# Decode attention with two branches on one core: normalization and output projection moved from the end into earlier heads

## The chip, the cores and the metric

The kernel runs on one core of one Trainium2 chip. The metric is the device time in microseconds (us); lower is better. The runs of one kernel lie close together (the twelve of the kernel before between 876.38 and 877.85 us, 0.2%), and most of the differences here lie between that and 1%. So kernels that are compared were timed in rounds against the kernel before, on the same chip.

A profile is one execution. Its span, from the first to the last instruction, is about 1.8 us shorter than the time measured for the same execution (2.4 us in one profiled run, `e6_same_pe_time`).

## The reference

There are two branches, A and B. Each is one decode step of attention with 32 heads of width 128, and each has its own input, caches and weights. A attends to all 16384 keys, B to the last 4096. The two results, 512 numbers each, are set side by side.

```python
def _A_ref(x, k_cache, v_cache, wq, wo):          # B is the same with
    ...                                           # k_cache[:, :, Sk - 4096:, :] and v alike
    q = (x @ wq).reshape(B, Sq, Hq, Dh).transpose(0, 2, 1, 3)
    scores = jnp.einsum("bhqd,bhkd->bhqk", q, k) * (Dh ** -0.5)
    p = _softmax(scores, axis=-1)
    o = jnp.einsum("bhqk,bhkd->bhqd", p, v)
    return o.transpose(0, 2, 1, 3).reshape(B, Sq, Hq * Dh) @ wo
...
return jnp.concatenate([a, b], axis=-1)
```

The K and V that must be read are 8 MB per A head and 2 MB per B head. With four weights of 4 MB, 336 MB go from memory into the core. (These MB are of 2^20 bytes; the profile counts in millions of bytes and shows 352.)

## The kernel before

A and B heads alternate: A0, B0, A1, B1, and so on, 64 in all; I call them heads 0 to 63, so that head 62 is the last A head and head 63 the last B head. A transfer brings one "unit", up to 64 blocks of 128 keys (2 MB), into a slot of a ring: five slots for K, four for V. All transfers go through one DMA queue, issued by SyncE (SP), and before each one SP waits until its slot is free.

For an A head PE transposes K in 16 groups of eight blocks, ACT copies each group from PSUM, and PE multiplies it with q. For a B head DVE forms the scores. ACT takes the exponential, and PE multiplies it with V (`ov`) in column `hidx` of the bank `OL[b]`; the sum of the exponentials goes to column 32 + `hidx`, in partition 0 only.

```python
for hh in range(NH):                       # PE
    ...
    if br == "A":
        for u in head_units[hh]:
            pe.wait_ge(s_k[ks], 16 * kocc[u])
            for gi in range(ugroups[u]):
                transposes(u, gi)
                if len(lag) >= 2:
                    scores(*lag.pop(0))
                lag.append((u, gi))
        while lag:
            scores(*lag.pop(0))
    if hh >= 1:
        ov(hh - 1)
ov(NH - 1)
```

Only after the last head are the sums inverted, broadcast by PE from partition 0 to all, copied and multiplied. Then come 32 products of 512 columns for A and 32 for B. A's output weights wo have lain in the weight buffer since head 6. B's wo (4 MB) is the last transfer of all and goes into two used slots of the K ring.

```python
# SP, after the last V
sp.dma_start(wob_view[:, :, :], B_wo.rearrange("(c p) n -> p c n", p=128)).then_inc(s_w, 16)
...
# PE, after the last head
pe.wait_ge(dve_m, DM_LINV)
...                                        # broadcast of the 64 inverse sums
pe.wait_ge(dve_m, DM_ONORM)
pe.wait_ge(s_w, 48)
for h in range(HQ):
    ins = pe.matmul(outA_ps, onorm[:, h : h + 1], wo_view[:, h, :], start=(h == 0), stop=(h == HQ - 1))
ins.then_inc(pe_fin, 1)
pe.wait_ge(s_w, 64)
for h in range(HQ):
    ins = pe.matmul(outB_ps, onorm[:, HQ + h : HQ + h + 1], wob_view[:, h, :], ...)
```

The softmax here doesn't subtract the row's maximum and nothing guards it: scores larger than these inputs give would overflow.

## Time and profile before

The time before was 877.49 us in three runs. The profiled run took 878.35 us, a little more than usual, with a span of 876.6 us.

| event before | us from the start |
|---|---|
| last V landed (all 16 completions) | 853.96 |
| attention of the last head done | 855.2 |
| last byte, B's wo: half of the completions, all 16 | 852.3, 864.75 |
| A's projection | 857.62 to 867.36 |
| B's projection | 867.36 to 874.28 |
| end of the span | 876.6 |

From the page of the kernel before: the busy share of the DMA engines and the rate they moved in 40 equal slices of 21.9 us, the queues (packets, MB, share of the 16 engines' time), and the chain of waits by engine.

```profile
span 876.6 us, 29290 instructions
DMA  7999799999999999999999999999999999999992
GB/s 289 422 428 384 300 385 425 426 424 424 422 424 424 424 425 423 426 425 424 423 424 425 424 424 425 425 424 423 420 425 410 423 422 422 408 425 413 419 360 77
q1 hardware_dynamic: 38082, 352.34, 96.3%
q8 instruction: 108, 1.77, 0.8%
DMA 79%; PE 14%; issue 3%; ACT 2%; DVE 2%; SPq 0%; ACTq 0%
```

The DMA engines are busy in nearly every slice, mostly at about 424 GB/s, and 79% of the chain is transfers. This kernel is limited by the bytes it reads: without B's wo the last V came 11.6 us earlier (`e4_no_wob`). Work of PE beside the transfers costs little (63 us more of it in the middle cost 0.7 us, `e6_same_pe_time`); what costs time is the work in the last slice, which moves 77 GB/s.

The end of the chain of waits before, in order of time (start, duration, what):

```profile
825.44 0.85 PE ol L483 x26
826.29 2.00 issue
828.29 1.18 PE ol L483 x38
...
829.98 23.98 DMA vring<-in_B_v_cache_dram
853.96 0.14 issue
854.10 0.99 PE ol L483 x32
...
857.62 9.74 PE misc L534 x32
867.36 6.92 PE misc L544 x32
874.28 0.02 issue
874.30 0.68 DVE out_sb L357
```

After the last V, 22.6 us pass, most of them in the two projections (L534 is A's, L544 is B's). B's products are faster: the granted clock rises from 0.5 to 1.0 at 863.06, and the starts of the products, 0.427 us apart before it, are then 0.216 us apart. B's wo is not in the chain: it landed at 864.75, while A's projection was running. The line of 2.00 us of "issue" in the middle of a run of 64 products: PE stood still there though the profile shows nothing that it waited for.

### The profile page before, as it was taken

The numbers are of one execution on the slowest core, as the hardware profiler recorded it, in microseconds if no ns is written. First come the engines' busy times: TensorE is split into PE (matmuls) and PEld (weight loads), VectorE is DVE, ScalarE is ACT, GpSimd is POOL, SyncE is SP. The second block draws the span as 40 slices with busy tenths as digits, with TensorE's granted clock in tenths as the row PEclk, the third lists the DMA queues.
The fourth block names the chain that finished last, engine by engine and source line by source line (L and its number), as shares of the span: only waits on it lengthen the run. The fifth ranks groups of instructions, "written<-read, shape, count | busy, mean of one in ns | idle before, by whom it ended". The sixth has DMA issues, their size and how long they took to land.

```text
span 876.6 us, 29290 instructions
## 1 busy us (share of the span) xinstructions
PE 648.8 (74%) x13764; PEld 569.8 (65%) x13764; DVE 223.8 (26%) x87; ACT 498.6 (57%) x641; POOL 0.7 (0%) x6
## 2 busy tenths in 40 slices
PE   1846885787777677778676787786767877777778
PEld 1745784676666666667665676776766766766673
DVE  0017303333112333331133333212333332123331
ACT  0603773677555556766555677655556776555660
POOL 0000000000000000000000000000000000000000
PEclk9956876788777688877677787766678786667778
DMA  7999799999999999999999999999999999999992
GB/s 289 422 428 384 300 385 425 426 424 424 422 424 424 424 425 423 426 425 424 423 424 425 424 424 425 425 424 423 420 425 410 423 422 422 408 425 413 419 360 77
DMA packets 38203, 354.21 MB, mean 404 GB/s; under 512 B 4289, under 2 KB 12481, under 8 KB 12482
## 3 DMA queue, kind: packets, MB, share of 16 engines
q1 hardware_dynamic: 38082, 352.34, 96.3%
q8 instruction: 108, 1.77, 0.8%
q14 instruction: 13, 0.11, 0.0%
HBM read 352.32 MB, written 0.00 MB: 402 GB/s over the span
## 4 chain that ended last, share of the span: by engine, by line
DMA 79%; PE 14%; issue 3%; ACT 2%; DVE 2%; SPq 0%; ACTq 0%
DMA vring<-in_A_v_cache_dram 72%; PE ol L483 7%; DMA wbuf<-in_B_wq_dram 3%; DMA vring<-in_B_v_cache_dram 3%; ACT kts L373 2%; PE misc L430 2%; DMA wbuf<-in_A_wq_dram 2%; PE ktp L447 1%; PE misc L534 1%; PE misc L544 1%; DVE qb_sb L300 1%; PE ol L491 1%; DVE sbb L324 1%; PE misc L409 0%; SPq L201 0%
## 5 line engine op out<-in xcount | busy, mean ns | idle before, releaser
L373 ACT ACTIVATE kts<-ktp 128x1024 bf16<-128x1024 bf16 x512 | 475.4, 1077 | 266.9 <-PE ktp L447 266.3
L447 PE MATMUL ktp<-ident,kring 128*128 128x128 bf16 x4096 | 361.8, 245 | 73.8 <-DMA kring<-in_A_k_cache_dram 73.4
L447 PEld LDWEIGHTS ktp<-ident,kring 128*128 128x128 bf16 x4096 | 286.2, 111 | 79.0 <-DMA kring<-in_A_k_cache_dram 76.9
L463 PE MATMUL sba<-qT_sb,kts 128*128 128x1 bf16 x4096 | 183.4, 166 | 69.9 <-ACT kts L373 42.2
L463 PEld LDWEIGHTS sba<-qT_sb,kts 128*128 128x128 bf16 x4096 | 149.4, 99 | 127.2 <-ACT kts L373 126.2
L315 DVE TENSOR_TENSOR prd<-kring,qb_sb 128x4096 bf16<-128x4096 bf16 x32 | 73.4, 2292 | 560.0 <-DMA kring<-in_B_k_cache_dram 559.8
L483 PE MATMUL ol<-ebuf,vring 128*128 128x1 bf16 x5120 | 150.8, 165 | 45.7 <-DMA vring<-in_A_v_cache_dram 35.3
L483 PEld LDWEIGHTS ol<-ebuf,vring 128*128 128x128 bf16 x5120 | 143.1, 103 | 50.0 <-DMA vring<-in_A_v_cache_dram 34.6
L324 DVE TENSOR_REDUCE sbb<-prd 128x32 f32<-128x4096 bf16 x32 | 141.4, 4420 | 1.1
L394 ACT ACTIVATE ebuf<-sbb 128x32 bf16<-128x32 f32 x32 | 7.3, 230 | 68.0 <-DVE sbb L324 52.1
L430 PE MATMUL misc<-wbuf,xrep 128*128 128x128 bf16 x128 | 15.1, 312 | 13.4 <-DMA wbuf<-in_B_wq_dram 7.9
L430 PEld LDWEIGHTS misc<-wbuf,xrep 128*128 128x128 bf16 x128 | 13.0, 146 | 15.3 <-DMA wbuf<-in_B_wq_dram 8.0
L381 ACT ACTIVATE ebuf<-sba 128x128 bf16<-128x128 f32 x32 | 8.9, 277 | 14.5 <-PE sba L463 14.5
L300 DVE CAST qb_sb<-misc 128x512 bf16<-128x512 f32 x8 | 5.5, 692 | 45.1 <-PE misc L430 45.1
L409 PE MATMUL misc<-xT_sb,wbuf 128*128 128x1 bf16 x128 | 3.6, 165 | 18.2 <-DMA wbuf<-in_A_wq_dram 18.2
L409 PEld LDWEIGHTS misc<-xT_sb,wbuf 128*128 128x128 bf16 x128 | 3.5, 104 | 18.2 <-issue 18.2
L491 PE MATMUL ol<-rowsum,ones_col 128*1 128x1 f32 x128 | 12.2, 164 | 3.1 <-issue 3.1
L534 PE MATMUL misc<-wbuf,onorm 128*1 128x512 bf16 x32 | 9.7, 479 | 0.7 <-DVE onorm L348 0.7
L534 PEld LDWEIGHTS misc<-wbuf,onorm 128*1 128x1 bf16 x32 | 3.1, 100 | 6.9 <-issue 3.9
L544 PE MATMUL misc<-kring,onorm 128*1 128x512 bf16 x32 | 7.1, 379 | 0.0
L491 PEld LDWEIGHTS ol<-rowsum,ones_col 128*1 128x1 f32 x128 | 5.5, 80 | 2.3 <-issue 1.3
L381 ACT ACTIVATION_READ_ACCUMULATOR ebuf<-sba 128x1 f32 x32 | 6.2, 194 | 0.0
(23 smaller groups left out, 16.6 us busy)
## 6 DMA issues: line engine op xcount, KB each, us to landing
kring<-in_A_k_cache_dram SPq DMA_DIRECT2D x64, 2048.0 KB, 28.5
vring<-in_A_v_cache_dram SPq DMA_DIRECT2D x64, 2048.0 KB, 22.6
kring<-in_B_k_cache_dram SPq DMA_DIRECT2D x32, 1024.0 KB, 28.8
vring<-in_B_v_cache_dram SPq DMA_DIRECT2D x32, 1024.0 KB, 33.6
wbuf<-in_A_wq_dram SPq DMA_DIRECT2D x1, 4096.0 KB, 13.6
wbuf<-in_B_wq_dram SPq DMA_DIRECT2D x1, 4096.0 KB, 29.5
wbuf<-in_A_wo_dram SPq DMA_DIRECT2D x1, 4096.0 KB, 31.4
kring<-in_B_wo_dram SPq DMA_DIRECT2D x1, 4096.0 KB, 34.2
```

The costliest lines, as they stand in the source:

```text
L300: v.tensor_copy(qb_sb[:, bch * 4 * DH : (bch + 1) * 4 * DH], misc7[:, 0 : 4 * DH],).then_inc(dve_m, 1)
L315: v.tensor_tensor(PRD[:, :].rearrange("p (c d) -> p c d", d=DH), Kring[:, ks * UC : ks * UC + TB, :], qb_bcast(hb), op=ALU.mult,).then_inc ...
L324: v.tensor_reduce(SBB[hb % 2][:, 0:TB], PRD[:, :].rearrange("p (c d) -> p c d", d=DH), AXX, ALU.add,).then_inc(dve_red, 1)
L373: act.activation(KTs[g % NS][:, 0 : GS * 128], KTP[g % NKB][:, 0 : GS * 128], ACTF.Copy,).then_inc(act_ev, 1)
L381: act.activation(Ebuf[e][:, 0:TA], SBA[:, 0:TA], ACTF.Exp, bias=0.0, scale=inv_sqrt_dh, accum_out=rowsum[e][:, 0:1],).then_inc(act_ex, 1)
L430: last = pe.matmul(misc7[:, i * DH : (i + 1) * DH], xrep[:, jc, :], wq_view[:, jc, hb * DH : (hb + 1) * DH], start=(jc == 0), stop=(jc == ...
L447: last = pe.transpose(KTP[g % NKB][:, t * 128 : (t + 1) * 128], Kring[:, ks * UC + c, :], ident[:, :],)
L463: last = pe.matmul(SBA[:, c0 + c : c0 + c + 1], KTs[g % NS][:, t * 128 : (t + 1) * 128], qT_sb[:, a_rank[hh] : a_rank[hh] + 1], start=True ...
L483: pe.matmul(OL[b][:, hidx : hidx + 1], Vring[:, vs * UC + c, :], Ebuf[e][:, c0 + c : c0 + c + 1], start=first, stop=(c0 + c == T - 1),)
L491: pe.matmul(OL[b][0:1, HQ + hidx : HQ + hidx + 1], ones_col[:, 0:1], rowsum[e][:, 0:1], start=True, stop=True,).then_inc(pe_ov, 1)
L534: ins = pe.matmul(outA_ps, onorm[:, h : h + 1], wo_view[:, h, :], start=(h == 0), stop=(h == HQ - 1),)
L544: ins = pe.matmul(outB_ps, onorm[:, HQ + h : HQ + h + 1], wob_view[:, h, :], start=(h == 0), stop=(h == HQ - 1),)
```

## The change

The intent is to leave nearly nothing after the last head. The sums are formed with a full 128x128 matrix of ones, so that each partition has them and the broadcast goes. Heads are normalized and projected in batches of eight. A's products run among the 16 groups of A heads 22, 38, 54 and 62, B's among those of 30, 46 and 62, and seven of B's within `ov` of head 62; only the last head of each branch is left for the end. B's wo comes in four transfers of 1 MB: three replace chunks of A's wo that are used up, after heads 22, 38 and 54, and the fourth is issued before the last three V transfers.

```diff
+                def issue_wob(k):
+                    if k < 3:
+                        sp.wait_ge(pe_pa, k + 1)
+                        dst = wo_view[:, k * CH : (k + 1) * CH, :]
+                    else:
+                        ...                      # wait for the last use of K slot 1
                 for hh in range(NH):
                     for u in head_units[hh]:
                         dma_k_unit(u)
+                    if hh == NH - 1:
+                        issue_wob(3)
+                    for k in range(3):
+                        if hh == 16 * k + 26:
+                            issue_wob(k)
...
-                sp.dma_start(wob_view[:, :, :], B_wo...)         # after the last V
...
                     pe.matmul(
-                        OL[b][0:1, HQ + hidx : HQ + hidx + 1],
-                        ones_col[:, 0:1],
+                        OL[b][:, HQ + hidx : HQ + hidx + 1],
+                        ones_mat[:, :],
                         rowsum[e][:, 0:1],
...
+                        if hh == NH - 2 and c0 > 0:              # in ov
+                            pe.wait_ge(dve_n, N_B3)
+                            pe.wait_ge(s_wb[3], 16)
+                            for h in range(3 * CH, HQ - 1):
+                                project(1, h)
...
+                for k in range(3):
+                    extra[16 * k + 22] = ([(dve_n, N_AB[k]), (s_w, 48)],
+                        [(0, h) for h in range(CH * k, CH * (k + 1))], True)
+                    extra[16 * k + 30] = ([(s_wb[k], 16)],
+                        [(1, h) for h in range(CH * k, CH * (k + 1))], False)
+                waits_, todo_, _f = extra[NH - 2]
+                extra[NH - 2] = (waits_ + [(dve_n, N_A3)],
+                    todo_ + [(0, h) for h in range(3 * CH, HQ - 1)], False)
...
                                 transposes(u, gi)
+                                if todo:
+                                    p = project(*todo.pop(0))
...
-                ...                              # broadcast, 32 products of A, 32 of B
+                pe.wait_ge(dve_n, N_A31)
+                project(0, HQ - 1).then_inc(pe_fin, 1)
+                pe.wait_ge(dve_n, N_B31)
+                project(1, HQ - 1).then_inc(pe_fin, 1)
```

## The prediction

> **What bounds it.** The DMA queue. The page's slices show the DMA engines at 0.9 or more in 37 of 40, mostly at about 424 GB/s; 79% of the chain of waits is DMA, and PE waits only 73 us for A's K and 35 us for A's V (waits). So the input stream ends when its bytes are in, whatever their order: the last packets end at 864.3 us. Half of the engines finish 12 us earlier (landings of the last transfer: 8th at 852.3, last at 864.8). The instruction queue (q8: 108 packets of 16 KB[...]) would explain that lag. The instruction count hardly changes, so I expect the lag to stay.
>
> **The end before.** B's wo (4 MB) comes last. The last V lands at 853.96; attention ends at 855.2; reciprocals, broadcast and scaling take until 857.6; A's projection 9.74 us, B's 6.92, the copy 0.68, the store and its receipt 1.6 (timeline, chain). So 22.6 us follow the last V, 12 us the last byte.
>
> **What changes.** The bytes stay, but V of the last head is now last: it should land where wo did, at 864.8, or up to 0.7 us later, because 1 KB packets take 51 instead of 46 ns while larger ones run (packets of the trace). 62 of the 64 projections move to earlier heads, where ACT paces PE (0.92 us per group against 0.65 of PE work) or PE waits for DMA. They cost 0.427 us each at half clock, 0.216 at full (starts of the 512-column products[...]). The DMA queue's new waits (projections of heads 22, 38, 54; last use of slot 1) are met before the queue reaches them, or with the wait beside them. The f32 sums over 128 columns cost about 0.5 instead of 0.19 us per head (estimate from the f32 broadcast, 0.53 each): +20 us of PE, hidden.
>
> **The new end.** K of the last A head lands some 26 us before the last V (23.7 before, plus 1 MB at 2.5 us), about 838.6. Its groups take 16.3 us plus 2 to 3 for 15 projections; then B's head 1.3, half of A's V 1.9, seven projections 1.5 to 3.0, the other half 1.9 + 0.5: 864.8 to 865.6. So PE and the last V (864.8 to 865.5) meet. Then last head 1.0, sum 0.5, normalization 0.5, projection 0.5, copy 0.7 (0.25 more behind A's copy on DVE), store 1.6: 870 to 871.5 of span. The measured time is 0.9 above the span: **predicted 871.2 us, 868.5 to 874.5 in 8 of 10**, a gain of 0.7%. Faster by over 2%: 0.01; within 2%: 0.97; slower: 0.02. About 17 of the 22.6 us go, but 11 come back, because the last V lands later.
>
> **Right or wrong.** Right if the last V lands at 864 to 866, the chain ends in it or in PE's last two heads, and DMA slices stay at about 424 GB/s. Wrong if the DMA has new holes after heads 26, 42, 58 or 63; if the last V lands before 862; or if PE's last A head takes over 3 us longer from its K than 16.3.
>
> **What could make it wrong.** A new stall near a wo chunk; a lower clock in the tail; another count of instruction packets on the lagging engines, which moves the end of the stream.

## The result, and the profile after

The changed kernel is correct. Its median is 873.53 us in ten runs (873.01 to 874.54) against 877.21 us. The ratio is 0.9958, with a 95% interval of 0.9949 to 0.9967: 0.4% faster, within 2%. The time lies in the predicted range, 2.3 us above the predicted value.

The same parts of the page for the changed kernel:

```profile
span 871.2 us, 29301 instructions
DMA  7999799999999999999999999999999999999995
GB/s 303 422 426 384 290 385 425 426 422 427 421 426 422 424 424 425 424 393 424 424 424 424 427 422 426 422 367 429 425 425 424 423 422 425 426 405 386 426 389 231
q1 hardware_dynamic: 38130, 352.34, 96.9%
q8 instruction: 108, 1.77, 0.8%
DMA 66%; PE 23%; ACT 4%; issue 4%; DVE 1%; SPq 1%; ACTq 0%
```

The bytes and the instruction packets are the same. The dips to 393, 367 and 386 GB/s are where the three chunks of wo pass. They are more than slow packets: in SP's timeline the transfer behind each chunk, a V of B, took 24.1, 22.1 and 23.2 us to issue, which the profile counts as issuing and not as a wait for a semaphore (0.43 us for the first of them in the run below without B's wo). Meanwhile the half of the DMA engines that is ahead (a reading of the completions, see "Which engines set the last byte") seems to have run out of work: the DMA share is 0.85 from 780 to 792 us, 1.01 in the kernel before. The half that is behind, which sets the last byte, went on: behind each chunk the ninth completion of V came 2.46 to 2.50 us after that of the chunk, as is usual for 1 MB (mostly 2.45 to 2.50 us in the kernel before). The last slice now carries 231 GB/s instead of 77: transfers go on nearly to the end. In the chain, PE has gained most of what the DMA lost.

The end of the chain in the changed kernel, with the head's K landing at its top:

```profile
811.75 28.11 DMA kring<-in_A_k_cache_dram
839.86 0.25 issue
840.11 1.01 PE ktp L482 x8
841.12 0.51 PE misc L508
...
845.78 0.47 PE ktp L482 x8
846.25 0.31 PE misc L508
846.56 0.28 PE sba L498 x8
...
857.95 1.03 ACT kts L408
858.98 0.05 issue
859.03 0.35 PE sba L498 x8
859.38 0.80 PE ol L535 x32
...
862.05 2.89 PE misc L508 x7
864.95 1.69 PE ol L535 x64
866.63 0.22 PE ol L543 x2
866.86 0.80 PE ol L535 x32
...
868.34 0.60 PE misc L508
868.96 0.68 DVE out_sb L392
```

From the landing of K at 839.86 to the end the chain is almost all PE's, with no further transfer in it. `misc L508` is a projection. One group of the last A head takes 0.47 + 0.31 + 0.28 = 1.06 us here; seven projections of B (2.89 us, at a granted clock of 0.5 until 864.63) stand between the two halves of A's V.

| us from the start, in the profiled runs | before | after |
|---|---|---|
| last V landed | 853.96 | 864.99 |
| last byte of any input | 864.75 | 864.99 |
| from the last V to the end | 22.6 | 6.2 |
| end of the span | 876.6 | 871.2 |

So 16.4 us of the tail went, and 11.0 us came back because the last V lands later: what used to come after it, B's wo, now comes before it. Where the last byte lands hardly moved. Of the remaining 5.4 us, 1.7 us are the sample: the profiled run before was 1.1 us above its median, and that of the changed kernel 0.5 us below its own. That leaves the 3.7 us between the medians.

### The profile page after: what moved, and what is told of

The parts are those of the page before. It is cut to its first block, busy times and chain, and to the rows that moved or that the text cites. A ratio compares the mean times of both kernels' runs of the same rounds, so it can differ in the third digit from the quotient of the medians. Undisturbed runs are those within 1.5% of the kernel's fastest.

```text
span 871.2 us, 29301 instructions
## 1 busy us (share of the span) xinstructions
PE 663.0 (76%) x13760; PEld 576.8 (66%) x13760; DVE 225.9 (26%) x100; ACT 503.7 (58%) x641; POOL 0.7 (0%) x6
## 2 busy tenths in 40 slices
DMA packets 38251, 354.21 MB, mean 407 GB/s; under 512 B 4337, under 2 KB 12529, under 8 KB 12530
## 4 chain that ended last, share of the span: by engine, by line
DMA 66%; PE 23%; ACT 4%; issue 4%; DVE 1%; SPq 1%; ACTq 0%
DMA vring<-in_A_v_cache_dram 40%; DMA kring<-in_A_k_cache_dram 21%; PE ol L535 7%; PE ktp L482 7%; ACT kts L408 4%; DMA wbuf<-in_B_wq_dram 3%; PE misc L508 3%; PE sba L498 2%; PE misc L465 2%; PE ol L543 2%; DMA wbuf<-in_A_wq_dram 1%; DVE qb_sb L342 1%; SPq L247 1%; DVE sbb L366 1%; PE misc L444 0%
## 5 line engine op out<-in xcount | busy, mean ns | idle before, releaser
L408 ACT ACTIVATE kts<-ktp 128x1024 bf16<-128x1024 bf16 x512 | 480.4, 1069 | 262.7 <-PE ktp L482 260.8
L482 PE MATMUL ktp<-ident,kring 128*128 128x128 bf16 x4096 | 357.7, 243 | 67.0 <-DMA kring<-in_A_k_cache_dram 62.8
L482 PEld LDWEIGHTS ktp<-ident,kring 128*128 128x128 bf16 x4096 | 281.1, 109 | 74.6 <-DMA kring<-in_A_k_cache_dram 51.6
L498 PEld LDWEIGHTS sba<-qT_sb,kts 128*128 128x128 bf16 x4096 | 146.5, 98 | 131.3 <-ACT kts L408 126.9
L535 PE MATMUL ol<-ebuf,vring 128*128 128x1 bf16 x5120 | 149.1, 165 | 40.5 <-DMA vring<-in_A_v_cache_dram 31.6
L535 PEld LDWEIGHTS ol<-ebuf,vring 128*128 128x128 bf16 x5120 | 146.6, 103 | 44.0 <-DMA vring<-in_A_v_cache_dram 28.2
L543 PE MATMUL ol<-rowsum,ones_mat 128*128 128x1 f32 x128 | 33.5, 331 | 0.0
L543 PEld LDWEIGHTS ol<-rowsum,ones_mat 128*128 128x128 f32 x128 | 29.5, 286 | 0.0
L508 PE MATMUL misc<-wbuf,onorm 128*1 128x512 bf16 x56 | 24.5, 438 | 0.0
L315 DVE RECIPROCAL linv<-ol 128x8 f32<-128x8 f32 (+2 forms) x10 | 2.0, 196 | 33.3 <-PE ol L543 33.3
L508 PEld LDWEIGHTS misc<-wbuf,onorm 128*1 128x1 bf16 x56 | 4.4, 79 | 7.4 <-issue 3.5
```

The lines of the kernel that those rows point to most:

```text
L408: act.activation(KTs[g % NS][:, 0 : GS * 128], KTP[g % NKB][:, 0 : GS * 128], ACTF.Copy,).then_inc(act_ev, 1)
L482: last = pe.transpose(KTP[g % NKB][:, t * 128 : (t + 1) * 128], Kring[:, ks * UC + c, :], ident[:, :],)
L498: last = pe.matmul(SBA[:, c0 + c : c0 + c + 1], KTs[g % NS][:, t * 128 : (t + 1) * 128], qT_sb[:, a_rank[hh] : a_rank[hh] + 1], start=True ...
L508: return pe.matmul((outA_ps, outB_ps)[b], onorm[:, b * HQ + h : b * HQ + h + 1], wo_view[:, h, :] if b == 0 else wob_head(h), start=(h == ...
L535: pe.matmul(OL[b][:, hidx : hidx + 1], Vring[:, vs * UC + c, :], Ebuf[e][:, c0 + c : c0 + c + 1], start=first, stop=(c0 + c == T - 1),)
L543: pe.matmul(OL[b][:, HQ + hidx : HQ + hidx + 1], ones_mat[:, :], rowsum[e][:, 0:1], start=True, stop=True,).then_inc(pe_ov, 1)
```

## The experiments

Twelve kernels were run. The questions were what sets the last byte's time, whether PE or the last V ends the changed kernel, which part of the change bought the time, and what limits a version without its weak points.

### PE's work in the last A head

```diff
-                waits_, todo_, _f = extra[NH - 2]
-                extra[NH - 2] = (waits_ + [(dve_n, N_A3)],
-                    todo_ + [(0, h) for h in range(3 * CH, HQ - 1)], False)
+                extra[NH - 4] = extra.pop(NH - 2)
...
+                        if hh == NH - 2:         # before the first transpose
+                            pe.wait_ge(dve_n, N_A3)
+                            for h in range(3 * CH, HQ - 1):
+                                project(0, h)
```

> The changed kernel with the 15 projections taken out of the last A head's groups: A's seven (heads 24 to 30) run before its first transpose, where PE waited 4.2 us for K, and B's eight of chunk 2 move one A head earlier. Theory 1 (PE ends the changed kernel, 2 us after the last V): the last A head's groups go back to about 16.3 us from 19.4, PE waits for the last V again, and the time falls by 1.0 to 1.8 us. Theory 2 (the last V alone sets the end, PE's extra work is hidden): no change, within 0.4 us.

Median 872.0 us, ratio to the kernel before 0.9945 (0.9933 to 0.9958), so about 1.1 us faster than the changed kernel. The two intervals overlap, so the size is uncertain; the profiled spans, 870.2 and 871.2 us, differ by about as much. In its timeline the groups of the last A head take 16.3 us, from 841.72 to 857.99, as expected. But the seven products before them ran from 838.64 to 841.79 and so past K's landing at 838.60, and the seven of B still took 3.1 us (granted clock 0.61 from 858 to 866). PE began the last head 0.9 us after its V had landed (865.99 against 865.13). The direction of theory 1 is supported: PE's late work was part of the end. The statement that PE waits for the last V again was not reached.

### B's wo at the end after all, in four transfers

A's early projections and all normalizations are kept. B's wo follows the last V as in the kernel before, but in four parts, and PE projects each part as it lands.

```diff
-                    if hh == NH - 1:
-                        issue_wob(3)
-                    for k in range(3): ...
...
+                for k in range(NCH):             # after the last V; NCH = 4, CW = 8
+                    sp.dma_start(wob_view[:, k * CW : (k + 1) * CW, :],
+                        B_wo[k * CW * DH : (k + 1) * CW * DH, :].rearrange("(c p) n -> p c n", p=128)
+                    ).then_inc(s_wb[k], 16)
...
                 pe.wait_ge(dve_n, N_B31)
-                project(1, HQ - 1)
+                for h in range(HQ - 1):
+                    if h % CW == 0:
+                        pe.wait_ge(s_wb[h // CW], 16)
+                    project(1, h)
+                project(1, HQ - 1)
```

A's products for heads 24 to 30 also run before the last A head's first transpose, as in the run above, so this is not the single part alone.

> One part of the change alone: A's projections and all normalizations early, but B's wo stays at the end of the stream as before, in four transfers of 1 MB, and B's projections follow at the end as each chunk lands. Theory 1 (bytes set the end of the stream, and only the work after the last byte counts): the last chunk lands at 864 to 866 as in both kernels, eight products of 0.22 to 0.43 us, copy and store follow, and the span ends at 869.5 to 871.5, as fast as the changed kernel or 1 us faster, so that moving B's wo forward gained nothing. Theory 2 (the gain comes from taking wo off the end of the stream): 2 us or more slower than the changed kernel.

Median 870.89 us, ratio 0.9933 (0.9919 to 0.9946): the fastest correct kernel, together with its variant below, and faster than the changed one, whose interval is 0.9949 to 0.9967. Against the run above the intervals overlap. The end of its chain:

```profile
853.17 11.27 DMA kring<-in_B_wo_dram
864.44 0.04 issue
864.48 1.90 PE misc L498 x8
866.39 0.02 issue
866.41 0.68 DVE out_sb L382
```

The last V lands at 853.17 (853.96 before), the last byte at 864.44 (864.75 before), and 4.3 us follow to the end at 868.7, a little below the span that theory 1 gave. Moving B's wo forward was therefore not needed. What counts is how little work stands behind the last byte, whichever tensor it belongs to.

### B's wo at the end, in one transfer

The same with `NCH = 1`.

> As the run with B's wo last in four transfers, but as one transfer of 4 MB, as in the kernel before, so that none of B's 32 products can start before its last byte. Theory 1 (only the work after the last byte counts): last byte at 864.8, then 32 products at 0.22 to 0.25 us, copy and store: a span of 873.5 to 875.5, so 2 to 3 us better than before and 5 us worse than in four transfers. Theory 2 (taking A's projection off the end gives its full 9.7 us): a span of 867 to 868.

Median 877.51 us, ratio 1.0005 (0.9991 to 1.0018): no gain over the kernel before. Both expectations missed. The end of its chain:

```profile
828.50 35.95 DMA kring<-in_B_wo_dram
864.45 0.14 issue
864.58 9.41 PE misc L498 x32
873.99 0.02 issue
874.02 0.68 DVE out_sb L382
```

The last byte is where theory 1 has it, but B's 32 products take 9.41 us where they took 6.92 us before. PE had been idle for 8.86 us before them. The granted clock had been 0.5 since 848.86, before this wait began, and stayed there until 869.34. In the kernel before it was at 0.5 from 845.99, but A's projection filled the wait, and the clock rose at 863.06.

### The same with a busy PE

```diff
                 pe.wait_ge(dve_n, N_B31)
+                for _t in range(26):             # results unused
+                    pe.matmul(OL[0][:, 0:512], ident[:, :], qb_sb[:, 0:512], start=True, stop=True)
```

> The run with B's wo last in one transfer, with 26 dummy products of 512 columns (into scratch PSUM) while PE waits some 9 us for wo. There the 32 products took 9.41 us, at a granted clock of 0.5 until 5 us after they began, where before they took 6.92 us. Theory 1 (PE's idle wait lowered its clock, and this ate what A's early projection had gained): the products take 6.9 to 7.3 us and the time falls by 2.1 to 2.5 us, to about 875.2. Theory 2 (wo's rows in the K ring or something else is slow): no change.

Median 876.21 us, ratio 0.9983 (0.9971 to 0.9996), by the ratios 1.9 us faster than without the dummy products. The chain's end:

```profile
828.47 36.08 DMA kring<-in_B_wo_dram
864.55 0.04 issue
864.60 7.08 PE misc L498 x32
```

The same 32 products now take 7.08 us, with the clock at 1.0 from 861.05. So the idle wait had kept the clock at half and taken back the gain of the early projection. It had not lowered the clock, as theory 1 has it: the clock fell at 848.86, 6.9 us before that wait began, with PE at work on the last heads (in the kernel before, where it fell at 845.99, PE had been busy 2.99 of the 4.00 us before that), and why it fell then is not shown. The rise came 4.0 to 5.5 us after the first of the products of 512 columns in six profiled runs: the kernel before, this one, and B's wo last in one part, in four equal parts and in the two uneven divisions below.

### Smaller last parts

```diff
-        NCH = 4
-        CW = HQ // NCH
+        WB = (0, 14, 24, 30, 32)
```

> The kernel with B's wo last, its four transfers cut as 14, 10, 6 and 2 heads instead of 8 each. Theory 1 (only the work after the last byte counts): 2 products instead of 8 follow the last byte, 0.5 to 0.9 us instead of 1.90, so 0.9 to 1.4 us faster than with four equal ones: a median of 869.5 to 870.1. Theory 2 (the last byte itself comes later with uneven chunks, or the clock drops while PE waits): no gain.

Median 872.38 us, ratio 0.9939 (0.9926 to 0.9953): no gain, theory 2. The first part, 14 heads, landed at 859.30 instead of 855.86. PE started 3.4 us later, with the products 0.43 us apart until 864.0, and ran all 32 without a pause in 9.29 us, until 868.73; the last byte at 865.63 no longer mattered.

With `WB = (0, 8, 16, 26, 32)`:

> The kernel with B's wo last, in transfers of 8, 8, 10 and 6 heads: the first ones as in the run with four equal ones, so that PE starts and warms as early as there, and 6 products in place of 8 after the last byte. Also a second sample of that version. Theory 1 (the small last chunk failed because the large first one let PE begin 3.4 us later, at half clock): as fast as four equal transfers or up to 0.5 us faster, a ratio to the kernel before of 0.9925 to 0.9940, the last 6 products in 1.3 to 1.5 us. Theory 2 (uneven chunks delay the last byte): about 1.2 us slower, as with 14, 10, 6 and 2.

Median 871.07 us, ratio 0.9927 (0.9913 to 0.9940). That agrees with four equal parts and is a second sample of that version on another occasion. Its profiled run was the slowest of its five (872.38 us): its last byte came at 866.64, and its last 16 products, which began at 864.67, took 3.63 us, so that the time of the last 6 alone can't be read.

### Bytes or work?

The changed kernel without any transfer of B's wo; B's products read A's wo, so B's result is wrong.

```diff
                 def issue_wob(k):
+                    return
...
-                            pe.wait_ge(s_wb[3], 16)
...
-                        [(s_wb[k], 16)],
+                        [],
...
-                        wo_view[:, h, :] if b == 0 else wob_head(h),
+                        wo_view[:, h, :],
```

> The changed kernel without any transfer of B's wo (B's products read A's wo: a wrong result for B on purpose). Theory 1 (bytes on the DMA set the time): 4 MB fewer, on the lagging engines 256 descriptors of 1 KB each at 43 to 47 ns, 11 to 12 us less. Theory 2 (the stream has slack, PE or the ring's waits set the pace): under 4 us less.

Median 864.64 us, ratio 0.9864 (0.9850 to 0.9877), by the ratios 8.2 us faster than the changed kernel. The last V landed at 853.36 instead of 864.99, 11.6 us earlier, as theory 1 says. The time fell less than its 11 to 12 us, because 9.4 us instead of 6.2 us followed the last V. Without the megabyte between them, the last A head's K and the last V come closer together (22.5 us apart instead of 25.1), and PE's chain from K to the end takes its time all the same. Again PE is last in this kernel.

### Which engines set the last byte

In the kernel before and in the one with B's wo in four parts, half of the completions of the last transfers come early. The last V of the kernel with B's wo in four parts had its first completion at 838.20, the eighth at 839.16 and the last at 853.17. The distance grows through the kernel, from about 1.5 us at 90 us to 15 us. I read the 16 completions of a transfer as one from each of the 16 DMA engines, so that half of the engines would be ahead of the others. The trace does not tell which engine moved a packet. The suspect was the fetching of instructions: 108 packets of 16 KB on the instruction queue, median 1.07 us each. (The kernel before has 27528 PE instructions, 255 for each packet.) My estimate: spread over eight engines that is 13.5 packets each, 14 us.

More instructions: 48 one-column products in each of 58 heads, in scratch columns.

```diff
+                    if 2 <= hh < NH - 4:
+                        for _t in range(48):
+                            pe.matmul(OL[b][:, 128:129], ident[:, :], Vjunk[:, 0:1], start=True, stop=True)
```

> The changed kernel with 48 added one-column products (scratch columns, results unused) in each of 58 heads: 2784 products, 5568 PE instructions, some 22 more instruction packets of 16 KB, about 1.4 us of PE per head. Theory 1 (the lag of half of the engines comes from the instruction packets, each costing its engine about 1.04 us, and the lagging engines set the end): 22/8 = 2.7 packets per lagging engine, so 2 to 3.5 us slower than the changed kernel, and a lag of 14 to 16 us instead of 12 where it is largest. Theory 2 (the lag has another cause): under 0.7 us slower.

The control, with the same time of PE in few instructions: `range(4)` and 384 columns.

> Control of the run before: four products of 384 columns in place of the 48, about the same PE time per head (1.3 us at half clock) in 464 PE instructions, 2 packets. Theory 1 (PE has slack in the middle): within 0.8 us of the changed kernel. Theory 2 (added PE time itself slows the stream by releasing buffers later): as slow as the run with 48 products.

The control ran 874.03 us (ratio 0.9966, 0.9953 to 0.9978), by the ratios 0.7 us slower than the changed kernel (the intervals overlap), with PE busy 726.0 us instead of 663.0 us. So PE's work in the middle is all but hidden. The kernel with more instructions ran 915.57 us (ratio 1.0444, 1.0424 to 1.0464), 42 us slower, which neither theory had. It has 129 instruction packets, and PE is busy 737.3 us, 11 more than in the control. What PE waited for in it (engine, line and what it waited for, us in total, times, longest), L545 being the product with V:

```profile
PEld ol L545 <- issue: 62.7, 29, 3.5
PE ol L545 <- issue: 59.9, 28, 3.5
PEld ktp L483 <- issue: 16.8, 20, 3.0
```

The same waits in the changed kernel:

```profile
PEld ktp L482 <- issue: 23.0, 20, 4.2
PEld ol L535 <- issue: 15.0, 12, 3.2
PE ol L535 <- issue: 8.4, 8, 2.2
```

PE stood idle 59.9 us in the middle of runs of products that wait for no semaphore, such as the 2.00 us of "issue" in the chain of the kernel before. Only the kernel with many small instructions has this to such an extent, and its control does not (3.2 us for PE on that line), so PE ran out of instructions; that is the plain reading, though the trace has no record of an instruction's arrival. The lag was no longer readable: the same bytes took 42 us longer, so the stream itself had pauses.

Fewer instructions, then: the kernel with B's wo in four parts, without every second product with V in heads 2 to 59 (wrong; all of V is still loaded).

```diff
+                            if 2 <= hh < NH - 4 and c % 2 == 1 and c0 + c != T - 1:
+                                continue
```

> The kernel with B's wo last in four transfers, without every second product with V in heads 2 to 59 (a wrong result on purpose; all V is still loaded): 2262 products and 4524 PE instructions fewer, 17 to 18 of the 108 instruction packets. The run with more instructions did not settle this, because PE stalled for instructions there. Theory 1 (each instruction packet takes about 1.04 us from one of 8 engines, and these engines set the end): 2.2 packets per lagging engine fewer, so 2 to 2.6 us faster than the four-transfer run, and the lag in the last transfers 11 to 12 us in place of 14.4 (the last V: first 838.2, last 853.2, less if the fast half waits). Theory 2 (lag from another cause): the same time within 0.7 us.

Median 867.7 us, ratio 0.9884 (0.9871 to 0.9898), with 90 packets. The last V landed at 850.55 instead of 853.17, the last byte at 861.73 instead of 864.44, and the span is 2.7 us shorter: by my estimate, 18 packets over eight engines at 1.07 us would be 2.4 us. By the ratios the gain is 4.3 us, more than the expected 2 to 2.6; the removed PE time may add up to the 0.7 us that the control showed, and the rest is not explained. The distance from the eighth to the last completion of the last V fell from 14.0 to 11.8 us; that from the first to the last, which was to fall to between 11 and 12 us, grew to 15.9 us, since the first completions came further ahead of the eighth (4.1 us instead of 1.0). So the size of the move of the last byte supports theory 1. The lag in mid-stream supports it too: in the transfer that landed at 543.78 in the kernel with B's wo in four parts, the eight late completions come on average 10.6 us after the eight early ones, and 66 instruction packets had passed; with fewer instructions, in the transfer landed at 541.55, it is 8.6 us after 55 packets. That it is exactly eight engines which fetch is inferred, not seen.

### Giving the slow half less to do

Two attempts to send B's wo through half of the engines only. First, each part in 16 transfers of 8 partitions, in the changed kernel. That such a transfer uses eight engines, always the same ("low" in the expectations), was my assumption; no run before had shown it:

```diff
-                    sp.dma_start(dst, B_wo[...].rearrange("(c p) n -> p c n", p=128)).then_inc(s_wb[k], 16)
+                    for p0 in range(0, 128, 8):
+                        sp.dma_start(dst[p0 : p0 + 8], src[p0 : p0 + 8]).then_inc(s_wb[k], 16)
```

> The changed kernel with each wo chunk of B sent as 16 transfers of 8 partitions. [...] Theory 1 (the stream's end is set by the 8 engines that lag, because they also fetch instructions): if the low engines are the fast half, the lagging half has 4 MB / 16 x 8 = 2 MB less to move, about 10 us (measured for wo of B at the end of the kernel before: 11 us on the lagging half), and the last V lands 3 to 8 us earlier, with PE's tail as far behind it; if the low engines are the lagging half, the last V lands about 10 us later. Theory 2 (all engines are limited together by one shared rate): the last V moves by less than 1.5 us.

Median 903.51 us, ratio 1.0306 (1.0292 to 1.0320), and neither theory was tested. The number of completions fits eight engines per transfer: 448 more packets under 512 B than with four transfers (4785 against 4337), and 64 x 8 - 4 x 16 = 448. But the queue was blocked. In SP's timeline the first 16 issues took from 353.89 to 385.48 us, 31.6 us, and no K or V could be issued meanwhile. The block is not the pieces' alone: in the changed kernel the one transfer takes 0.43 us, but the issue behind it 24.1 us. Slices of the transfer rate fell to 342 and 195 GB/s.

Second, in the kernel with B's wo last in four parts, a source of 8 by 16 rows for the last two:

```diff
+                        src = src.rearrange("(c a b) n -> a b c n", a=8, b=16)
```

> As the run with B's wo last in four transfers, but the last two with a source that is 8 by 16 rows, [...]in one transfer each (the pieces of 8 partitions of an earlier run blocked the queue instead). If so, the last two transfers show 8 completions each. Theory 1 with the low engines the fast half: the lagging half ends some 5.5 us earlier, and the span falls by 4 to 6 us to 863 to 865. With the low engines the lagging half: 5 us slower. If the access pattern is merged back to 128 rows: 16 completions, no change.

Median 871.37 us, ratio 0.9934 (0.9920 to 0.9947), with the same number of packets (38251) as without the edit: so no transfer had fewer completions, and the pattern was probably merged back to 128 rows. The landings of the first attempt suggest which half the pieces used. Of the 128 completions of the first chunk at least 57 came before 383.2 us, while the late half completed the transfer queued just before it from 383.27 on; so, if each engine takes its transfers in order (not shown here), the pieces went to the early half. Whether this can shorten the stream when the queue is not blocked stays open.

## Why the prediction was right, and where its terms were off

- **Right: bytes set the end of the stream, not their order.** The last V was to land at 864.8 to 865.5 and landed at 864.99. In the kernels with the same bytes and the same instructions the last byte came at 864.4 to 866.6. Without B's wo the last V came 11.6 us earlier.
- **Right: most of the saved tail comes back.** The prediction had about 17 us saved and 11 returned; the profiled runs show 16.4 and 11.0.
- **Right about the last byte, wrong about the lag.** The count of instruction packets stayed at 108, and the last byte hardly moved; removing 18 packets moved it by 2.7 us. Which engines fetch was not seen. But the lag was to stay, and it did not: from the eighth to the last completion of the last transfer it fell from 12.4 to 3.6 us, because the early completions stopped behind each piece of wo (next point).
- **Not foreseen: new holes.** The prediction named new holes of the DMA after heads 26, 42, 58 or 63 as a mark of being wrong. They are there: behind the four pieces of wo the first completion of the next transfer came 2.2 to 4.6 us later than its usual distance. They fell on the early half alone and cost next to nothing at the last byte (864.99 against 864.75). This was luck: the argument that the new waits are met in time covers the semaphores (no wait for the projections shows), not the time to issue.
- **Half right: PE and the last V were to meet.** PE came later. Its second half of A's V began at 864.95, 2.4 us after that V had landed (862.54), and the last head 1.9 us after the last V. K of the last A head landed at 839.86 instead of 838.6, and the groups then took 19.4 us. This is just past 16.3 plus 2 to 3, and at the bound of 3 us more which the prediction had named as another mark of being wrong.
- **Off: projections hidden where ACT paces PE.** That step of the argument took 0.216 us per projection at a granted clock of 1.0, which would have fitted beside ACT's 0.92 us per group. Between transposes and scores one took 0.31 us at the same clock, and the group 1.06 us: PE, not ACT, became the pace there. In the middle of the kernel this costs next to nothing, as the control with 63 us more of PE time shows. In the last A head it was part of the 3.1 us by which the groups grew, and removing it brought about 1.1 us.
- **Off: "the measured time is 0.9 above the span".** This compared the span of one profiled run with the median of other runs. The profiled run's own time was 878.35 us, so the difference is 1.8 us. With it, the prediction would have been 872.1 us. The rest of the 2.3 us is 0.9 us of span (871.2 against 870.3) and 0.5 us because the profiled run was faster than the median of its kernel.
- **Not foreseen: an alternative with the old order was better.** The prediction saw that the last byte stays, but not that B's wo may stay last if it comes in parts. That version ran 870.89 us, and its limit is now the stream itself plus 4.3 us.

## What to carry to other kernels

Where one queue streams all the input and half of the completions come without a pause to the end, as here, changing what comes last hardly changes when the last byte comes (864.4 to 866.6 us in the kernels with the same bytes and instructions): count only the work that must follow the last byte, and split the last transfer so that this work can start in parts. Moving work off the end can slow down what is left: with A's projection gone, the granted clock stayed at 0.5 through the wait that it used to fill, and B's 32 products took 9.41 us instead of 6.92; look at the granted clock of the tail before counting the gain. When a profile's span is turned into a time, use the time of that same execution, and at effects of half a percent take the before profile as one sample.

## What the runs show of instruction packets, small rows and issues

- Beside the stream, with 5568 more small PE instructions, PE was idle 59.9 us without a wait on one line, and the time grew by 42 us, while 63 us of PE time in 464 instructions cost 0.7 us (74 us in the 5568). That PE ran out of instructions is the plain reading, not a record of the trace.
- An instruction packet of 16 KB took 1.07 us (median) against 0.61 us for a data packet of that size, half of the completions came up to 14 us behind the others, and 18 packets fewer moved the last byte by 2.7 us.
- The rows of wo, 1 KB each, came at about 340 packets per us on all engines, 348 GB/s, where rows of 8 and 16 KB came at 424 GB/s.
- A copy of 8 partitions fits 8 completions (448 more in all). Issuing such copies can block the queue: 16 of them took 31.6 us to issue behind a full stream, the one transfer behind a 1 MB piece of wo took 22.1 to 24.1 us, and issuing the four 1 MB transfers of wo at the end took 27.8 us (which cost nothing there: the last byte came at 864.44).
